# The gates' rank chain of a top-2 mixture of experts: comparisons, maximum and subtraction on VectorE, counts, clipping and sum on GpSimd, the sum folded into the softmax's norm

## The chip, the cores and the metric

One core of a Trainium2 chip. The metric is the device time of one execution in microseconds; 617.84 us is the median of three runs of the kernel before.

## The reference

Inputs r, k, v, w, a, b are float32 [4, 8, 768, 40]. A recurrence over 768 steps gives y, which is laid out as x [4, 768, 320] and goes through a mixture of four attention experts of width 64. Per token the two experts with the largest gate logits count, weighted by a softmax over the two:

```python
def _moe_ref(x, w_gate, wq, wk, wv, wo):
    logits = x @ w_gate                                     # [B, S, 4]
    topk = np.argpartition(-logits, K, axis=-1)[..., :K]    # K = 2
    sel = np.take_along_axis(logits, topk, axis=-1)
    w = np.exp(sel - sel.max(-1, keepdims=True))
    w /= w.sum(-1, keepdims=True) + 1e-09
    for e in range(E):
        # q, k, v = x @ wq[e], x @ wk[e], x @ wv[e]; causal scores; softmax a
        ye = a @ v @ wo[e]
        # out += w of e, where e is one of the two, times ye
```

## The kernel before

The first part (up to about 375 us) computes the recurrence in chunks. The change does not touch it. The second part is the function moe. It works on 4 batches of 768 tokens; a batch has 6 tiles of 128 tokens, and its x comes in two halves of 384 tokens.

**What proj(b) gives per batch.** load (l, L708 to L710) fetches half of x from memory, in three transfers by SyncE's queue. split (s) makes a high and a low part of it: VectorE casts (L716), GpSimd subtracts twice (L717, L718). qk (k) makes the queries or keys of two experts for a half of the tokens: 8 matmuls (L739), a copy by ScalarE (L747), the rest by VectorE (L748), and for keys a transfer (L750). vg (v) makes the values and the gate logits of one tile (L758), which ScalarE copies out of PSUM (L761, and L762 into G[b], the tile "gg").

**The gates before.** rank (r; R for one half of the tiles) compares logit a with those after it on VectorE (L776, into "gc"); one slot later GpSimd adds each comparison to the later experts' counters and subtracts it from the earlier one's (L778, L780, the tile "gr"; set by four memsets, L773). Over a = 0, 1, 2 that makes nine GpSimd instructions. shift (h, H) takes the maximum on VectorE (L784), subtracts it on GpSimd (L785) and turns the counters into zeros and ones on VectorE (L786). gate (g, G) takes the exponential on ScalarE (L789), multiplies by the zeros and ones on GpSimd (L790), sums, adds 1e-9 and inverts on VectorE (L791 to L793) and multiplies on GpSimd (L794). Batch 0 does this by halves of three tiles, the other batches for all six at once, so there are five such chains.

**What a unit does.** A unit is one batch, one pair j of query tiles and one expert e; there are 48. scores: matmuls into PSUM (L816), mask addition and row minimum by VectorE (L823), exponential with its sum by ScalarE (L825). norm: VectorE adds 1e-9 to the sum (L830) and inverts it (L831), GpSimd multiplies by the gate (L832) and multiplies the two tiles of probabilities by that (L836). transp: TensorE transposes the probabilities (L844), ScalarE or VectorE copies them out of PSUM (L850, L848). mix: the product with the values (L862), copied by ScalarE and VectorE (L866, L867). fin: the output projection (L873), its copy (L876) and the store.

**What sets the order.** The program writes slots: the loop over units takes turns between scores, transposes, mixes and the pieces of the next batch's projection, which the strings FIRST, FILL0, FILL1 and FILL list; later(d, f) puts f d slots on (DL, DE, DN, DR). This part is not in manual order: the layer below places each engine's instructions, taking the program's order as the priority and its own idea of when inputs are ready, so that an engine's order in the trace can differ from the program's. Each engine executes its queue in order. Matmul outputs of "pt" share three PSUM buffers.

Of the kernel before, what the change touches and what calls it, by code (L numbers as in the profile page):

```python
# [14 lines left out]
AX = mybir.AxisListType  # L15
# [576 lines left out]

LAG = (3, 4, 6)

DL, DE, DN, DR = 1, 3, 4, 1

FIRST = "l1 k1 v0 k0 s1 v2 v1 R0 R1 R2 k2 H0 k3 G0"
FILL0 = "k4 k7", "k6 v4 k5", "v3", "v5 R3 R4 R5 H1", "G1", "", "", "", "", "", "", ""
FILL1 = "", "l0 s0", "", "", "l1", "k1 k0 s1", "v0 k2 v1 k3", "v3 v4", "v5 v2 k4", "", "r0 r1 k5", "r2 h g k6 k7"
FILL = "l0 s0 l1", "k3", "k0", "v0", "k1 k2", "s1", "v2 v1", "v5 v3 v4 r0", "k4", "r1 r2 k5", "k7 h g k6", ""  # L600
# [67 lines left out]
def moe(tc, ctx, I, xT, out, ident, pre, FL=None, FI=None):  # L668
    nc = tc.nc
    sp = ctx.enter_context(tc.tile_pool(name="moe", bufs=1, reuse_waits="tile"))  # L670
    pp = ctx.enter_context(tc.tile_pool(name="mps", bufs=1, space=PSUM, reuse_waits="tile"))
    V, A, T, PL = nc.vector, nc.scalar, nc.tensor, nc.gpsimd

    def f32(x):
        return x.bitcast(F32)
# [3 lines left out]
    def later(d, f):  # L679
        due.setdefault(now[0] + d, []).append(f)  # L680

    def slot(f):

        now[0] += 1
        for g in due.pop(now[0], []):
            g()
        f()

    def pj():
        return pp.tile([128, 512], F32, name="pt", tag="pt", bufs=3)  # L690
# [7 lines left out]
        A.activation(WS[0].rearrange("p k n -> p (k n)"), x, AF.Copy)  # L698
        V.tensor_tensor(WS[1].rearrange("p k n -> p (k n)"), x, h, op=OP.subtract)

    XH, XL, QS, KS, VV, G = {}, {}, {}, {}, {}, {}

    def load(b, n):

        t = slice(384 * n, 384 * n + 384)
        x = XL[b, n] = sp.tile([128, 3, 384], FR, name="x", bufs=2)
        x = f32(x)
        nc.sync.dma_start(x[:, 0:2], xT[b, 0:256, t].rearrange("(k p) t -> p k t", p=128))  # L708
        nc.sync.dma_start(x[0:64, 2], xT[b, 256:320, t])
        nc.sync.dma_start(x[64:128, 2], xT[b, 256:320, t])  # L710

    def split(b, n):
        l = XL[b, n]
        x = f32(l)
        h = XH[b, n] = sp.tile([128, 3, 384], FR, name="xh", bufs=2)
        V.tensor_copy(h, x)  # L716
        PL.tensor_tensor(h[64:128, 2], x[64:128, 2], f32(h[64:128, 2]), op=OP.subtract)  # L717
        PL.tensor_tensor(l[:, 0:2], x[:, 0:2], f32(h[:, 0:2]), op=OP.subtract)  # L718

    def products(w, x, b, n):  # L720

        h, l = XH[b, n], XL[b, n]
        return [(w[y][:, k], h[:, k]) for y in range(2) for k in range(2)] + [(w[y][:, 2], h[:, 2]) for y in range(2)] + \
               [(w[0][:, k], l[:, k]) for k in range(2)]

    def proj(b):
        wqk = [w.rearrange("p (k m n) -> p k m n", k=3, m=4) for w in WQ]
        wvg = [w.rearrange("p (k n) -> p k n", k=3) for w in WV]

        QS[b] = sp.tile([128, 4, 768], FR, name="qs", bufs=2)  # L730
        KS[b] = sp.tile([128, 4, 2, 768], FR, name="ks", bufs=2)
        VV[b] = sp.tile([128, 6, 4, 64], F32, name="vv", bufs=2)
        G[b] = sp.tile([128, 6, 4], F32, name="gg", bufs=2)
        def qk(m, n):
            def f():
                p = pj()[:, 0:384]
                prs = products([w[:, :, m] for w in wqk], None, b, n)
                for j, (w, x) in enumerate(prs):
                    T.matmul(p, w, x, start=(j == 0), stop=(j == len(prs) - 1))  # L739
                t = slice(384 * n, 384 * n + 384)  # L740
                for s in range(2):
                    e, o, x = 2 * (m % 2) + s, slice(64 * s, 64 * s + 64), slice(64 - 64 * s, 128 - 64 * s)
                    if m < 2:
                        h, l, c = QS[b][o, e, t], QS[b][x, e, t], -0.125
                    else:
                        h, l, c = KS[b][o, e, 0, t], KS[b][o, e, 1, t], 1.0
                    A.activation(h, p[o], AF.Copy, scale=c)  # L747
                    later(DL, lambda h=h, l=l, c=c, o=o: V.scalar_tensor_tensor(l, p[o], c, f32(h), op0=OP.mult, op1=OP.subtract))  # L748
                    if m >= 2:
                        later(DL, lambda e=e, o=o, x=x: nc.sync.dma_start(f32(KS[b][x, e, :, t]), f32(KS[b][o, e, :, t])))  # L750
            return f
        def vg(i):
            def f():
                n, c = divmod(i, 3)
                p = pj()[:, 0:260]
                prs = products(wvg, None, b, n)
                for j, (w, x) in enumerate(prs):
                    T.matmul(p, x[:, 128 * c:128 * c + 128], w, start=(j == 0), stop=(j == len(prs) - 1))  # L758
                v = VV[b][:, i]
                pv = p[:, 0:256].rearrange("p (e d) -> p e d", e=4)  # L760
                A.activation(v, pv, AF.Copy)  # L761
                A.activation(G[b][:, i], p[:, 256:260], AF.Copy)  # L762
            return f
        gs = {}
        def rank(a, i=slice(0, 6)):

            L = G[b][:, i]
            if a == 0:
                gs["R"] = sp.tile([128, 6, 4], F32, name="gr", bufs=2)
                gs["c"] = sp.tile([128, 3, 6, 3], F32, name="gc", bufs=1)  # L770
                gs["m"] = sp.tile([128, 2, 6], F32, name="gm", bufs=2)
                for d in range(4):
                    PL.memset(gs["R"][:, i, d], 3.0 - d)  # L773
            R, c = gs["R"][:, i], gs["c"][:, a, i]
            n = c.shape[1]
            V.tensor_tensor(c[:, :, 0:3 - a], L[:, :, a:a + 1].to_broadcast([128, n, 3 - a]), L[:, :, a + 1:4], op=OP.is_ge)  # L776
            def count():
                PL.tensor_tensor(R[:, :, a + 1:4], R[:, :, a + 1:4], c[:, :, 0:3 - a], op=OP.add)  # L778
                for d in range(3 - a):
                    PL.tensor_tensor(R[:, :, a], R[:, :, a], c[:, :, d], op=OP.subtract)  # L780
            later(DR, count)
        def shift(i=slice(0, 6)):
            L, R, mx = G[b][:, i], gs["R"][:, i], gs["m"][:, 0, i]
            V.tensor_reduce(mx, L, axis=AX.X, op=OP.max)  # L784
            PL.tensor_tensor(L, L, mx[:, :, None].to_broadcast(L.shape), op=OP.subtract)  # L785
            V.tensor_scalar(R, R, 1.5, None, op0=OP.is_lt)  # L786
        def gate(i=slice(0, 6)):
            L, R, mx, c = G[b][:, i], gs["R"][:, i], gs["m"][:, 0, i], gs["m"][:, 1, i]
            A.activation(L, L, AF.Exp)  # L789
            PL.tensor_tensor(L, L, R, op=OP.mult)  # L790
            V.tensor_reduce(mx, L, axis=AX.X, op=OP.add)  # L791
            V.tensor_scalar(mx, mx, 1e-9, None, op0=OP.add)
            V.reciprocal(c, mx)  # L793
            PL.tensor_tensor(L, L, c[:, :, None].to_broadcast(L.shape), op=OP.mult)  # L794
        half = lambda x: slice(3 * x, 3 * x + 3)
        return dict(l=lambda n: load(b, n), s=lambda n: split(b, n), k=lambda i: qk((0, 2, 1, 3)[i % 4], i // 4)(), v=lambda i: vg(i)(),
                    r=rank, h=lambda i: shift(), g=lambda i: gate(), R=lambda x: rank(x % 3, half(x // 3)),
                    H=lambda x: shift(half(x)), G=lambda x: gate(half(x)))

    OT, PT = {}, {}  # L800

    def unit(b, j, e, last):
# [24 lines left out]
                later(DN, norm)  # L827
        def norm():
            m = st["m"]
            V.tensor_scalar(m[:, 2], m[:, 1], 1e-9, None, op0=OP.add)  # L830
            V.reciprocal(m[:, 2], m[:, 2])  # L831
            PL.tensor_tensor(m[:, 3], m[:, 2], G[b][:, 2 * j:2 * j + 2, e], op=OP.mult)  # L832
            for t in range(2):
                n = 128 * (2 * j + t + 1)
                P = st["P"][t]
                PL.tensor_tensor(P[:, 0:n], P[:, 0:n], m[:, 3, t:t + 1].to_broadcast([128, n]), op=OP.mult)  # L836
# [149 lines left out]
```

## Time and profile before

| | |
|---|---|
| median of 3 runs | 617.84 us (616.05 to 618.46) |
| profiled execution, its own time | 615.63 us |
| its span, first to last instruction | 613.4 us |
| TensorE matmul busy | 537.8 us (88%), 8753 instructions |
| VectorE, ScalarE busy | 465.0 us, 469.8 us (76%, 77%) |
| GpSimd busy | 383.5 us (63%), 618 instructions |

The engines are PE (TensorE; PEld its weight loads), DVE (VectorE), ACT (ScalarE), POOL (GpSimd) and SP (SyncE). A row of the order of instructions gives the start in us, the time in us of the group, engine, line, operation, output<-input tiles, shape and count, and in brackets the idle time of the engine before it and who ended it. What matters below is where TensorE is idle, and which engine's wait ends last there.

### The profile page before, as it was taken

How to read it: one execution, taken by the hardware profiler on the slowest of the kernel's cores; microseconds unless marked ns; L12 is line 12 of the kernel's file. 1: busy time of each engine (PE TensorE's matmuls, PEld its weight loads, DVE VectorE, ACT ScalarE, POOL GpSimd, SP SyncE). 2: the span in 40 equal slices, each digit the busy share in tenths (PEclk: the TensorE clock that was granted, in tenths of full speed). 3: DMA queues.
4: the chain of work that ended last, by engine and by line, in shares of the span. 5: the costliest groups of instructions: out<-in, count | busy, mean ns of one | idle time of the engine just before them, and what ended most of it. 6: DMA issues, size and time to landing. Idle time of an engine off the chain costs nothing.

```text
span 613.4 us, 22296 instructions
## 1 busy us (share of the span) xinstructions
PE 537.8 (88%) x8753; PEld 473.7 (77%) x8753; DVE 465.0 (76%) x1142; ACT 469.8 (77%) x1272; POOL 383.5 (63%) x618
## 2 busy tenths in 40 slices
PE   5554589998898899889899999889999889999996
PEld 5554588887777788778788888778988778887884
DVE  7978868899989999997676584777885477567752
ACT  7992479899878988987889985667775567677773
POOL 2421089859988988998984630685763746363851
PEclk9555589999999999999999999999999989999998
DMA  7885244576477557746925845222221131102101
GB/s 189 214 192 135 95 112 123 134 196 161 117 181 196 154 129 206 166 101 173 229 85 157 216 119 162 76 79 66 83 77 48 40 91 59 59 2 57 45 36 52
DMA packets 63690, 73.77 MB, mean 120 GB/s; under 512 B 30168, under 2 KB 48344, under 8 KB 63576
## 3 DMA queue, kind: packets, MB, share of 16 engines
q1 hardware_dynamic: 63432, 72.15, 45.4%
q8 instruction: 72, 1.18, 0.8%
q14 instruction: 42, 0.34, 0.2%
q10 hardware_dynamic: 144, 0.10, 0.1%
HBM read 54.92 MB, written 11.01 MB: 107 GB/s over the span
## 4 chain that ended last, share of the span: by engine, by line
PE 53%; ACT 16%; POOL 11%; DVE 10%; issue 7%; DMA 2%; SPq 1%; POOLq 0%; DVEq 0%; ACTq 0%
PE py L415 6%; PE ot L862 6%; PE pt L739 5%; PE sc L816 4%; PE pt L844 4%; PE pt L873 4%; POOL MT L319 4%; PE pt L441 3%; PE ps L392 3%; POOL TP L319 3%; PE ps L405 3%; PE ps L383 3%; PE pt L758 3%; PE pt L372 2%; ACT GT L386 2%
## 5 line engine op out<-in xcount | busy, mean ns | idle before, releaser
L319 POOL TENSOR_TENSOR MT<-MT,TP 128x30 f32<-128x30 f32 (+9 forms) x150 | 98.2, 654 | 11.6
L319 POOL TENSOR_TENSOR TP<-MT 128x30 f32<-128x30 f32 (+9 forms) x150 | 93.6, 624 | 11.4
L836 POOL TENSOR_TENSOR P<-P,m 128x128 f32<-128x128 f32 (+2 forms) x96 | 89.0, 948 | 3.5
L415 PE MATMUL py<-R,LS 128*40 128x80 f32 x1536 | 83.5, 236 | 1.9 <-DVE R L408 0.4
L823 DVE CUSTOM_DVE_ANT_0 P<-sc,MK 128x128 f32<-128x128 f32 (+2 forms) x96 | 59.5, 622 | 23.6 <-PE sc L816 13.9
L825 ACT ACTIVATE P<-P,m 128x128 f32<-128x128 f32 (+2 forms) x96 | 63.8, 665 | 11.5 <-DVE m L823 10.7
L415 PEld LDWEIGHTS py<-R,LS 128*40 128x40 f32 x1536 | 63.0, 118 | 8.6 <-ACT LS L445 3.6
L408 DVE TENSOR_TENSOR R<-ps,CM 64x128 f32<-64x128 f32 x192 | 55.0, 286 | 16.3 <-PE ps L405 12.3
L816 PE MATMUL sc<-ks,qs 128*128 128x384 f32 (+4 forms) x256 | 61.5, 345 | 2.0 <-DVE m L823 1.9
L394 ACT ACTIVATE R<-ps 32x160 f32<-32x160 f32 x192 | 56.6, 295 | 5.3 <-PE ps L392 1.2
L386 ACT ACTIVATE GT<-ps 32x160 f32<-32x160 f32 x192 | 56.4, 294 | 3.7 <-PE ps L383 0.3
L832 POOL TENSOR_TENSOR m<-m,gg 128x2 f32<-128x2 f32 x48 | 10.3, 214 | 78.0 <-DVE m L831 54.7
L844 PE MATMUL pt<-CM,P 128*128 128x128 f32 x336 | 52.5, 277 | 6.2 <-ACT pt L850 5.1
L445 ACT ACTIVATE LS<-pt 40x320 f32<-40x320 f32 x92 | 39.6, 430 | 12.6 <-PE pt L441 9.3
L392 PE MATMUL ps<-GT,TT 128*33 128x80 f32 x768 | 46.7, 242 | 2.7 <-issue 1.0
L376 ACT ACTIVATE LS<-pt 64x320 f32<-64x320 f32 x96 | 41.4, 432 | 9.7 <-PE pt L372 8.2
L844 PEld LDWEIGHTS pt<-CM,P 128*128 128x128 f32 x336 | 40.1, 141 | 11.2 <-ACT pt L850 6.2
L405 PE MATMUL ps<-RB,VU 128*64 128x64 f32 x768 | 46.0, 228 | 2.0 <-ACT VU L400 1.5
L816 PEld LDWEIGHTS sc<-ks,qs 128*128 128x128 f32 x256 | 40.8, 191 | 4.2 <-DVE m L823 3.4
L739 PE MATMUL pt<-xh,wq 128*128 128x384 f32 x192 | 41.6, 349 | 2.1 <-DVE xh L716 1.2
L283 PE MATMUL ps<-AB,KB 40*64 40x32 f32 x512 | 26.1, 273 | 19.0 <-DVE AB L258 12.8
L441 PE MATMUL pt<-CM,R 104*104 104x104 f32 x368 | 42.4, 258 | 0.0
(160 smaller groups left out, 1337.6 us busy)
## 6 DMA issues: line engine op xcount, KB each, us to landing
RB<-in_RB SPq DMA_DIRECT2D x24, 320.0 KB
EK<-in_EK SPq DMA_DIRECT2D x18, 416.0 KB
ks<-ks SPq DMA_DIRECT2D x32, 192.0 KB
R<-in_VG SPq DMA_DIRECT2D x24, 208.0 KB
EW<-in_EA SPq DMA_DIRECT2D x18, 214.5 KB
R<-in_VT SPq DMA_DIRECT2D x48, 80.0 KB
R<-in_RT SPq DMA_DIRECT2D x24, 160.0 KB
xT<-XT SPq DMA_DIRECT2D x48, 80.0 KB
```

The lines of the kernel that those rows point to most:

```text
L319: return [lambda: e.tensor_tensor(tmp, row, col, op=OP.mult), lambda: e.tensor_tensor(o, o, tmp, op=OP.add)]
L386: A.activation(gt[b:b + 32, s::2], p_g[64 * s:64 * s + 32], AF.Copy)
L392: T.matmul(p_u[64 * x:64 * x + 33, y], tt[:, o:o + 33], gt[:, 2 * p:2 * p + 2], start=True, stop=True, tile_position=(0, 64 * x))
L405: T.matmul(p_f[64 * x:64 * x + 64, y], vu[:, p, :], rb[:, 4 * g + p, :], start=True, stop=True, tile_position=(0, 64 * x))
L415: T.matmul(py[64 * s:64 * s + 40, p], ls[:, h, :], m, start=True, stop=True, tile_position=(0, 64 * s))
L441: T.transpose(PT[0:104, P // 4, 104 * (P % 4):104 * (P % 4) + 104], rn[0:104, o:o + 104], ident[0:104, 0:104])
L739: T.matmul(p, w, x, start=(j == 0), stop=(j == len(prs) - 1))
L816: T.matmul(ps[:, c, 0:cw], QS[b][:, e, o], KS[b][:, e, z, k], start=(z == 0), stop=(z == 1))
L823: V.tensor_tensor_reduce(pv, ps[:, 0:ch, 0:cw], MK[:, 768 - n:768].rearrange("p (c k) -> p c k", c=ch), 1.0, 3e38, OP.add, OP.min, m[:, 0, ...
L825: later(DE, lambda: A.activation(P[:, 0:n], P[:, 0:n], AF.Exp, bias=m[:, 0, t:t + 1], scale=-1.0, accum_out=m[:, 1, t:t + 1]))
L836: PL.tensor_tensor(P[:, 0:n], P[:, 0:n], m[:, 3, t:t + 1].to_broadcast([128, n]), op=OP.mult)
L844: T.transpose(p[:, 128 * y:128 * y + 128], st["P"][t][:, 128 * c:128 * c + 128], ident)
```

## The change

- rank keeps only the comparison; the counters start at d - 1 and not at 3 - d, and the delay DR is gone.
- shift takes the maximum and subtracts it on VectorE, takes the exponential on ScalarE at once, and then does all nine counts on GpSimd, with the signs turned round, and clips the counters to 0 and 1 there (max(min(R, 1), 0)).
- gate is GpSimd's alone: product, two additions for the sum over four experts, and an instruction that adds 1e-9 and writes the sum to a new tile "gt" (GS[b], two buffers). The gates are no longer divided by their sum.
- norm multiplies the softmax's sum (plus 1e-9) by that sum of the gates before it inverts, in place of adding 1e-9 alone.
- The tiles "gr" and "gm" have one buffer and not two.
- FIRST, the order of batch 0's first pieces, has v1 k2 k3 v2 and then the ranks, where it had v2 v1, the ranks, and k2 and k3 among the rest.

```diff
-DL, DE, DN, DR = 1, 3, 4, 1
-FIRST = "l1 k1 v0 k0 s1 v2 v1 R0 R1 R2 k2 H0 k3 G0"
+DL, DE, DN = 1, 3, 4
+FIRST = "l1 k1 v0 k0 s1 v1 k2 k3 v2 R0 R1 R2 H0 G0"
...
+        GS[b] = sp.tile([128, 6], F32, name="gt", bufs=2)
         def rank(a, i=slice(0, 6)):
...
-                gs["R"] = sp.tile([128, 6, 4], F32, name="gr", bufs=2)
+                gs["R"] = sp.tile([128, 6, 4], F32, name="gr", bufs=1)
                 gs["c"] = sp.tile([128, 3, 6, 3], F32, name="gc", bufs=1)
-                gs["m"] = sp.tile([128, 2, 6], F32, name="gm", bufs=2)
+                gs["m"] = sp.tile([128, 2, 6], F32, name="gm", bufs=1)
                 for d in range(4):
-                    PL.memset(gs["R"][:, i, d], 3.0 - d)
...
+                    PL.memset(gs["R"][:, i, d], d - 1.0)
+            c = gs["c"][:, a, i]
+            V.tensor_tensor(c[:, :, 0:3 - a], L[:, :, a:a + 1].to_broadcast([128, c.shape[1], 3 - a]), L[:, :, a + 1:4], op=OP.is_ge)
         def shift(i=slice(0, 6)):
             L, R, mx = G[b][:, i], gs["R"][:, i], gs["m"][:, 0, i]
             V.tensor_reduce(mx, L, axis=AX.X, op=OP.max)
-            PL.tensor_tensor(L, L, mx[:, :, None].to_broadcast(L.shape), op=OP.subtract)
-            V.tensor_scalar(R, R, 1.5, None, op0=OP.is_lt)
+            V.tensor_tensor(L, L, mx[:, :, None].to_broadcast(L.shape), op=OP.subtract)
+            A.activation(L, L, AF.Exp)
+            for a in range(3):
+                c = gs["c"][:, a, i]
+                PL.tensor_tensor(R[:, :, a + 1:4], R[:, :, a + 1:4], c[:, :, 0:3 - a], op=OP.subtract)
+                for d in range(3 - a):
+                    PL.tensor_tensor(R[:, :, a], R[:, :, a], c[:, :, d], op=OP.add)
+            PL.tensor_scalar(R, R, 1.0, 0.0, op0=OP.min, op1=OP.max)
         def gate(i=slice(0, 6)):
-            A.activation(L, L, AF.Exp)
+            L, R, t, g = G[b][:, i], gs["R"][:, i], gs["m"][:, :, i], GS[b][:, i]
             PL.tensor_tensor(L, L, R, op=OP.mult)
-            V.tensor_reduce(mx, L, axis=AX.X, op=OP.add)
-            V.tensor_scalar(mx, mx, 1e-9, None, op0=OP.add)
-            V.reciprocal(c, mx)
-            PL.tensor_tensor(L, L, c[:, :, None].to_broadcast(L.shape), op=OP.mult)
+            PL.tensor_tensor(t.rearrange("p k i -> p i k"), L[:, :, 0:2], L[:, :, 2:4], op=OP.add)
+            PL.tensor_tensor(g, t[:, 0], t[:, 1], op=OP.add)
+            PL.tensor_scalar(g, g, 1e-9, 1.0, op0=OP.add, op1=OP.mult)
...
         def norm():
             m = st["m"]
-            V.tensor_scalar(m[:, 2], m[:, 1], 1e-9, None, op0=OP.add)
+            V.scalar_tensor_tensor(m[:, 2], m[:, 1], 1e-9, GS[b][:, 2 * j:2 * j + 2], op0=OP.add, op1=OP.mult)
             V.reciprocal(m[:, 2], m[:, 2])
```

## Rows read from the trace of the kernel before

**Rows 1.** Stretches: length, busy PE PEld DVE ACT POOL, PEclk, DMA share, GB/s.
```profile
396.00:404.00 8.00, 5.21 (x34) 4.13 (x32) 4.62 (x22) 4.92 (x18) 7.28 (x24) 1.00 0.44 125
432.00:480.00 48.00, 47.24 (x347) 41.42 (x347) 34.75 (x86) 33.38 (x83) 26.81 (x33) 1.00 0.25 72
493.80:497.30 3.50, 3.50 (x16) 3.50 (x15) 2.42 (x9) 3.05 (x8) 2.03 (x4) 0.51 0.02 5
```

**Rows 2.** Order of instructions: the memsets of the counters of batch 0.
```profile
370.09 0.32 POOL L773 MEMSET gr<- 128x3 f32 x8 [3.44 <-PE ps L392]
```

**Rows 3.** Waits from 376 us on: who for whom; us, times, longest.
```profile
ACT gg L789 <- POOL gg L785: 9.2, 4, 4.4
DVE gr L786 <- POOL gr L780: 8.6, 4, 3.6
```

**Rows 4.** Order of instructions, TensorE: idle times near the five gate chains.
```profile
384.99 0.77 PE L739 MATMUL pt<-xh,wq 128*128 128x384 f32 x3 [1.21 <-DVE xh L716]
...
388.21 0.62 PE L739 MATMUL pt<-x,wq 128*128 128x384 f32 x2 [1.27 <-DVE gm L792]
...
404.09 0.73 PE L816 MATMUL sc<-ks,qs 128*128 128x512 f32 x2 [1.65 <-DVE m L823]
...
427.34 0.55 PE L844 MATMUL pt<-CM,P 128*128 128x128 f32 x3 [1.04 <-ACT pt L850]
...
492.35 0.55 PE L844 MATMUL pt<-CM,P 128*128 128x128 f32 x3 [3.67 <-ACT pt L850]
...
549.18 0.55 PE L844 MATMUL pt<-CM,P 128*128 128x128 f32 x3 [0.38 <-ACT pt L850]
```

**Rows 5.** Order of instructions, VectorE and GpSimd: batch 0's first half.
```profile
383.97 0.17 DVE L786 TENSOR_SCALAR gr<-gr 128x12 f32<-128x12 f32 x1 [1.60 <-POOL gr L780]
384.08 0.76 DVE L716 CAST xh<-x 128x1152 fp32r<-128x1152 f32 x1
...
385.26 1.01 POOL L717 TENSOR_TENSOR xh<-x,xh 64x384 fp32r<-64x384 f32 x1
386.34 1.81 POOL L718 TENSOR_TENSOR x<-x,xh 128x768 fp32r<-128x768 f32 x1
```

**Rows 6.** The same: batch 0's second half.
```profile
400.67 0.97 POOL L836 TENSOR_TENSOR P<-P,m 128x128 f32<-128x128 f32 x2
...
403.26 0.17 DVE L786 TENSOR_SCALAR gr<-gr 128x12 f32<-128x12 f32 x1 [2.58 <-POOL gr L780]
...
405.56 0.14 DVE L830 TENSOR_SCALAR m<-m 128x2 f32<-128x2 f32 x1
```

**Rows 7.** The same, GpSimd and ScalarE: batch 1.
```profile
423.20 2.68 POOL L836 TENSOR_TENSOR P<-P,m 128x640 f32<-128x640 f32 x2
...
426.44 0.22 ACT L789 ACTIVATE gg<-gg 128x24 f32<-128x24 f32 x1 [1.73 <-POOL gg L785]
```

**Rows 8.** The same: batch 2, with TensorE's instructions that come next.
```profile
489.13 0.53 POOL L780 TENSOR_TENSOR gr<-gr,gc 128x6 f32<-128x6 f32 x3
...
489.87 0.22 ACT L789 ACTIVATE gg<-gg 128x24 f32<-128x24 f32 x1 [4.41 <-POOL gg L785]
...
491.99 1.82 POOL L836 TENSOR_TENSOR P<-P,m 128x384 f32<-128x384 f32 x2
...
495.17 1.08 PE L844 MATMUL pt<-CM,P 128*128 128x128 f32 x4
...
504.64 0.86 PE L816 MATMUL sc<-ks,qs 128*128 128x320 f32 x4
```

**Rows 9.** Lines L830, L776 (ns min/median/max); VectorE beside GpSimd, batch 1.
```profile
L830 DVE TENSOR_SCALAR m<-m x48: 126/169/1426, 391.2 to 599.7; 128x2 f32<-128x2 f32 x48
L776 DVE TENSOR_TENSOR gc<-gg x15: 151/164/626, 382.0 to 544.9; 128x6 f32<-128x6 f32 x5, 128x18 f32<-128x18 f32 x3, 128x12 f32<-128x12 f32 x3, 128x9 f32<-128x9 f32 x2
...
429.67 1.01 POOL L717 TENSOR_TENSOR xh<-x,xh 64x384 fp32r<-64x384 f32 x1
...
429.73 0.98 DVE L792 TENSOR_SCALAR gm<-gm 128x6 f32<-128x6 f32 x1
```

More of the change, by code (lines that the diff above doesn't have):

```diff
@@ L699, in split_wo @@
         V.tensor_tensor(WS[1].rearrange("p k n -> p (k n)"), x, h, op=OP.subtract)
-    XH, XL, QS, KS, VV, G = {}, {}, {}, {}, {}, {}
+    XH, XL, QS, KS, VV, G, GS = {}, {}, {}, {}, {}, {}, {}
     def load(b, n):
@@ L768, in rank @@
             if a == 0:
-                gs["R"] = sp.tile([128, 6, 4], F32, name="gr", bufs=2)
+                gs["R"] = sp.tile([128, 6, 4], F32, name="gr", bufs=1)
                 gs["c"] = sp.tile([128, 3, 6, 3], F32, name="gc", bufs=1)
-                gs["m"] = sp.tile([128, 2, 6], F32, name="gm", bufs=2)
+                gs["m"] = sp.tile([128, 2, 6], F32, name="gm", bufs=1)
                 for d in range(4):
-                    PL.memset(gs["R"][:, i, d], 3.0 - d)
[L774 to L781, printed above, removed]
+                    PL.memset(gs["R"][:, i, d], d - 1.0)
+            c = gs["c"][:, a, i]
+            V.tensor_tensor(c[:, :, 0:3 - a], L[:, :, a:a + 1].to_broadcast([128, c.shape[1], 3 - a]), L[:, :, a + 1:4], op=OP.is_ge)
         def shift(i=slice(0, 6)):
@@ L784, in shift @@
             V.tensor_reduce(mx, L, axis=AX.X, op=OP.max)
-            PL.tensor_tensor(L, L, mx[:, :, None].to_broadcast(L.shape), op=OP.subtract)
-            V.tensor_scalar(R, R, 1.5, None, op0=OP.is_lt)
+            V.tensor_tensor(L, L, mx[:, :, None].to_broadcast(L.shape), op=OP.subtract)
[6 more added lines that the diff above has]
+            PL.tensor_scalar(R, R, 1.0, 0.0, op0=OP.min, op1=OP.max)
         def gate(i=slice(0, 6)):
-            L, R, mx, c = G[b][:, i], gs["R"][:, i], gs["m"][:, 0, i], gs["m"][:, 1, i]
-            A.activation(L, L, AF.Exp)
+            L, R, t, g = G[b][:, i], gs["R"][:, i], gs["m"][:, :, i], GS[b][:, i]
             PL.tensor_tensor(L, L, R, op=OP.mult)
-            V.tensor_reduce(mx, L, axis=AX.X, op=OP.add)
-            V.tensor_scalar(mx, mx, 1e-9, None, op0=OP.add)
-            V.reciprocal(c, mx)
-            PL.tensor_tensor(L, L, c[:, :, None].to_broadcast(L.shape), op=OP.mult)
+            PL.tensor_tensor(t.rearrange("p k i -> p i k"), L[:, :, 0:2], L[:, :, 2:4], op=OP.add)
+            PL.tensor_tensor(g, t[:, 0], t[:, 1], op=OP.add)
+            PL.tensor_scalar(g, g, 1e-9, 1.0, op0=OP.add, op1=OP.mult)
         half = lambda x: slice(3 * x, 3 * x + 3)
```

## The prediction

> **What bounds the kernel now.** I read the stretches of the attention part first, then the trace's order of instructions, then the waits, then TensorE's idle times, and last the instructions around each of the five places where gates are computed. In the stretches [rows 1] the reader should see that TensorE is the bound wherever no gate is computed: 47.24 us busy of 48.00 from 432 to 480. Where gates are computed it is not: 5.21 of 8.00 from 396 to 404. So a microsecond of idle TensorE removed there is a microsecond off the end, as long as nothing else is late at the same place.
>
> [Rows 2] show that the trace's order is not the program's: the memsets of both halves' counters run at 370.09, though the second half's stand several units further down in the program. The layer that builds this part places an instruction where it thinks its inputs are ready, earlier program lines first. The order after the change can therefore only be argued, not read off the diff.
>
> The waits [rows 3] name the price of the gates today. ScalarE waits 9.2 us, four times, with its exponential of the gates for GpSimd's subtraction of the maximum. VectorE waits 8.6 us, four times, with the comparison on L786 for GpSimd's counts. Everything behind these two in the queues waits too: copies of transposes out of PSUM (L850), mask additions of scores (L823), the cast of the next x (L716). TensorE's idle times [rows 4] lie just there: 1.21 + 1.27 in the start, 1.65 for the second half of batch 0, 1.04, 3.67 and 0.38 for batches 1, 2 and 3; 9.22 together. After the 3.67 the granted clock is 0.51 over 493.8 to 497.3 [rows 1], that is nearly all at the lower level, 1.2 GHz; over 396 to 404, and so up to the idle time of 1.65, it was 1.00, 2.4 GHz.
>
> **The change part by part.** *Start of batch 0* [rows 5]. The cast of the second half of x ran at 384.08, right behind L786, which had waited 1.60 for GpSimd. L786 is gone, and the ranks move behind v2 in the program, so the cast can start when VectorE is free, at 383.97 - 1.60 = 382.37, 1.7 earlier, and some 0.4 more since the three comparisons and the maximum no longer stand ahead of it. I take 2.0. GpSimd's two splits of x (1.01 and 1.81) follow the cast, and TensorE's wait at 388.21 ends with the second, at 388.15; both come 2.0 earlier. The bounds are 0 (x's load may land as late as the cast; no row shows its landing) and 2.48, the two idle times themselves. I take 2.0 since L786's wait ended within 0.11 us of the cast. The order v1, k2, k3, v2 is the same TensorE work: 0.
>
> *Second half of batch 0* [rows 6]. VectorE stood from 400.68 to 403.26 before L786, while the mask addition that TensorE waits for stood behind it. Without L786 it starts some 2 us earlier, TensorE had nothing else from 402.44: 1.65 gained, bounds 0 and 1.65. *Batch 1* [rows 7]. The exponential stood 1.73 before 426.44, until GpSimd had done a pair of probabilities of 2.68; it now waits for VectorE's own subtraction, so the copy behind it, and TensorE's 1.04, are free. Bounds 0 and 1.04; I take 1.04, since TensorE's next input, that pair, was ready at 425.88.
>
> *Batch 2* [rows 8]. The exponential waited from 485.46 to 489.87. From its start to TensorE's next transposes, which want the copy behind it, is 492.35 - 489.87 = 2.48 [rows 4, 8]. If it starts at 486.3 they can run at 488.8; TensorE left off at 492.35 - 3.67 = 488.68, so almost all of the 3.67 goes. Next late is GpSimd: its counts end at 489.13 + 0.53 = 489.66; clip, product, two sums and the final scaling take five more at about 0.2 (three counts take 0.53), to 490.7, where today it passes through the subtraction, two waits on other engines and L794, and starts the next pair at 491.99. That pair can start at 490.9 and end at 492.7 instead of 493.81. TensorE's transposes that want it, at 495.17 today, would be reached near 491 and wait to 492.7: 2.5 gained. A wait of 1 to 2 us is nearer to the 1.65 that left the clock at 1.00 than to the 3.67, so I count the clock as kept: from 495.17 to 497.3 some 2.1 us of work at half rate give back 1.0. Together 3.5; bounds 1.1 (GpSimd's own gain) and 5.4 (3.67, and half of 3.5 at the lower clock). *Batch 3*: 0.38, bounds 0 and 0.38 [rows 4].
>
> *What is added.* GpSimd has two instructions more for each of five gates (clip, two sums, final scaling; less the subtraction and one product): 5 x 2 x 0.2 = 2.0 us, beside TensorE's work except in batch 2, where it is in the sum; bounds 0 and 2.0. The counters' single buffer keeps the next memset behind the product that frees it; both are GpSimd's, so no engine waits. VectorE loses five instructions per gate and gains one subtraction. The norm's L830 becomes an instruction with two tensors: its median is 169 ns and that of L776, also two tensors on few columns, 164 [rows 9]: 0. It adds one wait: every norm now needs the gates' sum from GpSimd, and behind it in VectorE's queue stand mask additions and copies. For batch 2 the first norm that reads its sum comes after its first scores, at 504.64 [rows 8], over 10 us after the sum. For the second half of batch 0 it is close: GpSimd is through with a pair at 400.67 + 0.97, counts (1.5) and five more (1.0) make 404.2, and the norm of the first unit that needs it ran at 405.56 [rows 6]. Both move up, the norm by 1.65 more, which makes a wait of 0.3 at most: 0, bound 0.3.
>
> [Rows 9] also show VectorE's two-input and plain instructions stretched while GpSimd works: L792 took 0.98 inside GpSimd's 1.01. By that, VectorE's new subtraction can be stretched by as much as one GpSimd instruction, which is why I let batch 2's exponential start at 486.3 and not at 485.46 and the 0.2 of a subtraction: half a split like that of 1.81 [rows 5] may lie before it. The Trainium skill, page "SBUF — State Buffer", section "Who interferes with whom", says that a VectorE instruction with two SBUF inputs and a GpSimd instruction that reads SBUF exclude each other; by that rule the stretch is a full block, in all five places. The trace agrees: L776, with two such inputs, takes up to 0.626 where its median is 0.164; what it would cost here is a rival below.
>
> **The sum**: 2.0 + 1.65 + 1.04 + 3.5 + 0.38 = 8.6 us. The profiled execution took 615.63 (span 613.4), so its successor would take 607.0, span about 604.8. The median of the three runs, 617.84, is 2.2 above it; off the median the forecast is 609.2.
>
> **Rivals.** *GpSimd counts first.* The layer puts the start's counts ahead of the x split, so the reordering does not do what it says. The ranks stand behind v2, whose matmuls end where TensorE left off today, 383.78; counts from about 384.9, 1.5 + 0.2, then 1.01 + 1.81: TensorE's wait ends near 389.5, 1.3 later than now and not 2.0 earlier. Gain 8.6 - 3.3 = 5.3: 612.5. For it: today's order has the counts ahead of the split; against it: the split is now much earlier in the program than the counts.
>
> *The block.* VectorE's subtraction waits out a GpSimd instruction in all five places, near 0.9 each (half of a split, 1.81 [rows 5]): gain 8.6 - 4.5 = 4.1: 613.7. Against it: batch 2's delay is in the sum already. The rule that speaks for it is that of the Trainium skill, page "SBUF — State Buffer", named above.
>
> *Nothing to be had.* Where the stall goes, the next input is just as late: GpSimd's pairs of probabilities, or the placing differs and puts a like idle elsewhere. What stays is GpSimd's 1.1 in batch 2 and about 0.9 in batch 1: 615.8. For it: GpSimd is busy 7.28 of 8.00 around 400 [rows 1].
>
> *The wait is only renamed (slower).* VectorE now stands at the norm for GpSimd's sum as long as it stood at L786. This decides if GpSimd takes the gates' block behind the next pair of probabilities (2.68 [rows 7]) so that the sum comes after VectorE has reached a norm that reads it, the second half of batch 0 above all. Then nothing is gained, two more GpSimd instructions in five places cost 2.0, and one pair 2.7: 622.5. Against it: batches 1 to 3 have their sums long before.
>
> **How the numbers follow.** Forecast 0.58; counts first 0.11; the block 0.08; nothing 0.14; renamed 0.09. The likeliest gives 609.2. Its own range is 606 (nearly all upper bounds: 2.48 + 1.65 + 1.04 + 5.4 + 0.38 = 10.95, and 1 for a better order) to 613. The whole range reaches up to 616.5, which takes in 612.5, 613.7 and 615.8, and leaves out 622.5; down to 605.5. A measurement here can tell about 0.5%, 3.1 us: under 614.8 is faster, 0.58 + 0.11 + 0.08 = 0.77; same 0.14; slower 0.09.
>
> **What would show it.** Right: no wait of ScalarE's exponential or VectorE on GpSimd's gates; TensorE's idle before 388 and near 402 and 426 gone; near 490 at most 2 us, with the clock at 1.00. Wrong in the start: the cast still follows the comparisons, or GpSimd's split follows counts. Wrong in batch 2: TensorE still idle 3 us or more. Wrong in sign: VectorE's norm waits for a tile of gates' sums, several us in all.

## The result, and the profile after

The changed kernel is faster by 1.0%: 610.99 us, the median of 20 runs, against 617.0 for the kernel before on the same chips (20 runs); the ratio is 0.9901, with a 95% interval of 0.9879 to 0.9923. That is 6.0 us by the medians, where the forecast was 8.6. The single executions lie between 606.12 and 616.06. The ratios, here and in the table of the experiments, leave out executions over 1.5% above the fastest of the same kernel (one of the 20 of after, five of the 12 of "clip only", one each of "old order" and of "the same, subtraction apart"), while the medians hold all.

| | before | after |
|---|---|---|
| median of 20 runs, us | 617.0 | 610.99 |
| span of the profiled execution, us | 613.4 | 610.7 |
| start of the last matmul of the recurrence (L415) in it | 374.8 | 376.4 |
| from there to the end of the span | 238.6 | 234.3 |

The profiled pair shows less than the medians, and the last two rows say in part why. The recurrence, which the change does not touch, took 1.6 us more in the execution shown of after: behind the stretch from 15 to 81 us, nearly all of it at 0.5 in both, TensorE's granted clock fell to 0.5 there twice, for 3.4 us at 264.1 and at 308.5, and never in the one shown of before. So I compare the part behind the recurrence, which I call *the tail* (the expectations below call it the part after the attention): 238.6 and 234.3 us, 4.3 us less. Where the rest of the 6.0 lies no trace shows. Where in the tail the time went is seen from when a given matmul of the mix (L861, L862 before) starts, counted from the last one of the recurrence:

| start of the mix matmul number | 1 | 121 | 145 | 345 | end of the span |
|---|---|---|---|---|---|
| before | 30.62 | 104.94 | 127.29 | 219.57 | 238.57 |
| after | 28.91 | 102.78 | 124.00 | 215.48 | 234.32 |
| gained so far | 1.7 | 2.2 | 3.3 | 4.1 | 4.3 |

Number 1 lies behind TensorE's idle times at both halves of batch 0's gates, number 121 behind batch 1's, number 145 behind batch 2's and number 345 behind batch 3's. From 121 to 145, over the gates of batch 2, which were to bring 3.5, the gain is 1.1.

The page of the kernel after; the first row is busy time, share of the span and instructions of each engine, the second the granted clock in 40 slices:

```profile
PE 540.2 (88%) x8753; PEld 475.8 (78%) x8753; DVE 467.3 (77%) x1127; ACT 469.5 (77%) x1272; POOL 384.7 (63%) x628
...
PEclk9555589999999999989989999999999989999999
```

Stretches of the kernel after: length, busy PE PEld DVE ACT POOL, PEclk, DMA share, GB/s:

```profile
396.00:404.00 8.00, 6.82 (x47) 5.74 (x45) 7.05 (x28) 6.33 (x23) 7.30 (x18) 1.00 0.54 145
432.00:480.00 48.00, 47.28 (x350) 41.44 (x350) 33.88 (x84) 33.67 (x84) 27.54 (x32) 1.00 0.25 72
489.40:492.80 3.40, 3.40 (x17) 2.52 (x16) 3.25 (x10) 3.04 (x10) 2.57 (x11) 0.50 0.01 2
```

They answer to [rows 1]. Around batch 0's second half TensorE is now busy for 6.82 of 8.00 us, where it was 5.21. From 432 to 480 nothing changed, as nothing should. Behind batch 2's gates the clock is still at its lower level, 1.2 GHz: 0.50 for 3.4 us.

Waits of the kernel after from 376 us on: who for whom, line that wrote it; us, times, longest:

```profile
DVE m L829 <- POOL gt L793: 2.3, 2, 2.0
ACT gg L781 <- DVE gg L780: 2.3, 2, 1.8
```

These are what is left of [rows 3]. ScalarE's 9.2 us for GpSimd's subtraction and VectorE's 8.6 us for GpSimd's counts have no successors among the waits for gates; instead VectorE's norm waits twice for the gates' sum, and ScalarE twice for VectorE's subtraction.

TensorE in the kernel after, its idle times of over 0.4 us in the tail (start, busy time, engine, line, instruction, idle time before it and what ended it):

```profile
386.12 0.41 PE L739 MATMUL pt<-xh,wq 128*128 128x384 f32 x1 [0.74 <-DVE xh L716]
...
389.08 0.61 PE L739 MATMUL pt<-x,wq 128*128 128x384 f32 x2 [1.20 <-POOL x L718]
...
393.59 0.96 PE L758 MATMUL pt<-wv,xh 128*128 128x260 f32 x6 [0.66 <-DVE qs L748]
...
399.39 0.99 PE L758 MATMUL pt<-wv,xh 128*128 128x260 f32 x6 [0.47 <-ACT gg L762]
...
403.98 0.73 PE L815 MATMUL sc<-ks,qs 128*128 128x512 f32 x2 [0.55 <-DVE m L822]
...
414.44 0.63 PE L843 MATMUL pt<-CM,P 128*128 128x128 f32 x4 [0.41 <-POOL P L835]
...
488.44 0.73 PE L815 MATMUL sc<-ks,qs 128*128 128x512 f32 x2 [2.04 <-DVE m L822]
...
497.96 0.79 PE L739 MATMUL pt<-xh,wq 128*128 128x384 f32 x3 [0.60 <-DVE pt L847]
...
553.17 1.31 PE L739 MATMUL pt<-xh,wq 128*128 128x384 f32 x6 [0.60 <-DVE pt L847]
```

Beside [rows 4]: 1.21 and 1.27 became 0.74 and 1.20, with 0.66 new behind them; 1.65 became 0.55; 1.04 and 0.38 are gone; 3.67 became 2.04, and what it waits for is new: not ScalarE's copy but VectorE's mask addition (L822). The 0.60 at 497.96 is new too. An idle time of before that [rows 4] do not show, ahead of the 1.65, is gone as well:

```profile
399.92 0.33 PE L844 MATMUL pt<-CM,P 128*128 128x128 f32 x1 [0.61 <-POOL P L836]
```

VectorE of the kernel after in the start:

```profile
384.06 1.12 DVE L748 SCALAR_TENSOR_TENSOR qs<-pt,qs 64x384 fp32r<-64x384 f32 x2 [0.39 <-ACT qs L747]
385.22 0.76 DVE L716 CAST xh<-x 128x1152 fp32r<-128x1152 f32 x1
...
391.92 0.16 DVE L829 SCALAR_TENSOR_TENSOR m<-m,gt 128x2 f32<-128x2 f32 x1 [1.97 <-POOL gt L793]
```

Against [rows 5] the cast no longer follows a wait for GpSimd, but it follows a split of qs; and the first norm stands 1.97 us for the gates' sum. The cast did not stand for x's load: in the trace each transfer raises a semaphore 16 times as it lands, and by these counts the last of the load's three had landed at 383.95, 1.27 us ahead of the cast (before: 381.54, cast at 384.08).

VectorE and GpSimd at the 2.04, batch 2 of the kernel after (its three comparisons are one row), and TensorE's scores that the mask addition of 512 columns takes up:

```profile
480.71 0.16 DVE L829 SCALAR_TENSOR_TENSOR m<-m,gt 128x2 f32<-128x2 f32 x1 [1.28 <-ACT P L824]
480.95 0.76 DVE L716 CAST xh<-x 128x1152 fp32r<-128x1152 f32 x1
481.63 0.16 DVE L830 RECIPROCAL m<-m 128x2 f32<-128x2 f32 x1
...
484.05 3.65 DVE L776 TENSOR_TENSOR gc<-gg 128x18 f32<-128x18 f32 x3
487.62 0.17 DVE L779 TENSOR_REDUCE gm<-gg 128x6 f32<-128x24 f32 x1
487.70 0.67 DVE L822 CUSTOM_DVE_ANT_0 P<-sc,MK 128x512 f32<-128x512 f32 x1
488.31 0.08 DVE L822 DVE_READ_ACCUMULATOR2_ANT m<- 128x1 f32 x1
488.31 0.23 DVE L780 TENSOR_TENSOR gg<-gg,gm 128x24 f32<-128x24 f32 x1
...
481.95 1.01 POOL L717 TENSOR_TENSOR xh<-x,xh 64x384 fp32r<-64x384 f32 x1 [1.72 <-DVE m L830]
483.04 0.20 POOL L831 TENSOR_TENSOR m<-m,gg 128x2 f32<-128x2 f32 x1
483.19 1.85 POOL L718 TENSOR_TENSOR x<-x,xh 128x768 fp32r<-128x768 f32 x1
484.99 2.68 POOL L835 TENSOR_TENSOR P<-P,m 128x640 f32<-128x640 f32 x2
487.63 0.22 POOL L784 TENSOR_TENSOR gr<-gr,gc 128x18 f32<-128x18 f32 x1
...
483.50 0.71 PE L815 MATMUL sc<-ks,qs 128*128 128x512 f32 x2
```

The same comparisons in the kernel before, with GpSimd's order there, and in batch 3 of the kernel after:

```profile
484.59 0.79 DVE L776 TENSOR_TENSOR gc<-gg 128x18 f32<-128x18 f32 x3
...
481.98 3.20 POOL L836 TENSOR_TENSOR P<-P,m 128x640 f32<-128x640 f32 x2
485.26 1.02 POOL L717 TENSOR_TENSOR xh<-x,xh 64x384 fp32r<-64x384 f32 x1
...
543.10 0.34 DVE L776 TENSOR_TENSOR gc<-gg 128x18 f32<-128x18 f32 x3
```

The three comparisons are the same instructions as before, and took 3.65 us where they had taken 0.79. Taken one by one they run 484.05 to 485.07, 484.99 to 486.27 and 486.19 to 487.69. GpSimd's x split ends at 485.04, and its pair of probabilities is two instructions that end at 486.24 and 487.67: each comparison ends with one GpSimd instruction. Behind them stand the mask addition, whose scores had been done since 484.21, and, behind that, TensorE.

### The profile page after: what moved, and what is told of

Its sections match the earlier page's. It is cut to its first block, busy times and chain, and to the rows that moved or that the text cites. A ratio compares the mean times of both kernels' runs of the same rounds, so it can differ in the third digit from the quotient of the medians.

```text
span 610.7 us, 22319 instructions
## 1 busy us (share of the span) xinstructions
PE 540.2 (88%) x8753; PEld 475.8 (78%) x8753; DVE 467.3 (77%) x1127; ACT 469.5 (77%) x1272; POOL 384.7 (63%) x628
## 4 chain that ended last, share of the span: by engine, by line
PE 53%; POOL 16%; DVE 13%; ACT 9%; issue 6%; DMA 2%; SPq 1%; DVEq 0%; POOLq 0%; ACTq 0%
POOL MT L319 7%; POOL TP L319 7%; PE ot L861 6%; PE py L415 6%; PE pt L739 5%; PE sc L815 5%; PE pt L843 4%; PE pt L872 4%; PE pt L441 4%; PE pt L758 3%; PE ps L392 3%; PE ps L405 3%; PE ps L383 3%; PE pt L372 2%; PE ps L399 2%
## 5 line engine op out<-in xcount | busy, mean ns | idle before, releaser
L415 PE MATMUL py<-R,LS 128*40 128x80 f32 x1536 | 84.0, 238 | 2.2 <-DVE R L408 0.4
L822 DVE CUSTOM_DVE_ANT_0 P<-sc,MK 128x128 f32<-128x128 f32 (+2 forms) x96 | 59.3, 623 | 24.1 <-PE sc L815 12.4
L415 PEld LDWEIGHTS py<-R,LS 128*40 128x40 f32 x1536 | 63.6, 119 | 8.7 <-ACT LS L445 3.6
```

The lines of the kernel that those rows point to most:

```text
L415: T.matmul(py[64 * s:64 * s + 40, p], ls[:, h, :], m, start=True, stop=True, tile_position=(0, 64 * s))
L822: V.tensor_tensor_reduce(pv, ps[:, 0:ch, 0:cw], MK[:, 768 - n:768].rearrange("p (c k) -> p c k", c=ch), 1.0, 3e38, OP.add, OP.min, m[:, 0, ...
```

## The experiments

The theory that I took into the runs: the waits went as foretold, and batch 2 lost its gain since VectorE's comparisons are held by GpSimd's instructions. Its rivals: the new order of the start does the work; the fold (norm times the gates' sum) costs what the rest gains; what is left is set by x's load. The table holds all runs. Ratios are against runs of the kernel before on the same chip, whose medians were 617.99 to 619.18 beside the other kernels, and are not the quotients of two medians; "idle" is TensorE's first idle time over 0.5 us around batch 2's gates, "clock" whether the granted clock fell to 0.5 there.

| kernel | median | ratio (95%) | tail | idle | clock | three comparisons |
|---|---|---|---|---|---|---|
| before | 617.0 | | 238.6 | 3.67 | fell | 0.79 |
| after | 610.99 | 0.9901 (0.9879 to 0.9923) | 234.3 | 2.04 | fell | 3.65 |
| order only | 618.98 | 1.0002 (0.9969 to 1.0035) | 240.6 | 3.67 | fell | 0.77 |
| old order | 612.94 | 0.9868 (0.9818 to 0.9919) | 237.2 | 2.23 | fell | 3.83 |
| comparisons on GpSimd | 616.98 | 0.996 (0.9929 to 0.9991) | 237.8 | 2.80 | fell | on GpSimd |
| the same, subtraction apart | 611.36 | 0.9899 (0.9869 to 0.9929) | 234.5 | 0.83 | kept | on GpSimd |
| not folded | 611.2 | 0.9872 (0.9821 to 0.9924) | 233.3 | 0.93 | kept | 0.88 |
| inverted by GpSimd | 610.32 | 0.9897 (0.9855 to 0.9938) | 231.1 | 0.80 | kept | 0.74 |
| subtraction only | 616.2 | 0.9974 (0.9939 to 1.0009) | 235.9 | 2.56 | fell | 0.76 |
| clip only | 617.81 | 0.9961 (0.9921 to 1.0001) | 237.8 | 3.54 | fell | 0.66 |
| wo later | 613.48 | 0.9921 (0.9887 to 0.9955) | 233.9 | 0.75 | kept | 2.35 |
| inverted, wo later | 610.0 | 0.9851 (0.9801 to 0.9901) | 232.8 | 0.72 | kept | 0.65 |
| inverted, compared on GpSimd, apart | 611.66 | 0.9893 (0.9854 to 0.9932) | 230.9 | 0.93 | kept | on GpSimd |

The tail is one execution's, and a fall of the clock in the start alone moves it: "order only" has one at 406.7, "old order" one of 6.8 us at 387.9.

**Comparisons on GpSimd.** After, with this edit:

```
-            V.tensor_tensor(c[:, :, 0:3 - a], ..., L[:, :, a + 1:4], op=OP.is_ge)
+            PL.tensor_tensor(c[:, :, 0:3 - a], ..., L[:, :, a + 1:4], op=OP.subtract)
+            PL.tensor_scalar(c[:, :, 0:3 - a], c[:, :, 0:3 - a], 0.0, None, op0=OP.is_ge)
```

> The changed kernel with its three comparisons per gate chain taken off VectorE: GpSimd subtracts and compares with 0, so two GpSimd instructions stand for one of VectorE's (six for three). Theory (the block): VectorE's comparisons, with two inputs in SBUF, stood behind GpSimd's instructions for 3.65 us in batch 2 and 1.94 us in the start, and TensorE's idle 2.04 us near 488 with the low clock behind it comes from that. Then the mask addition of 512 columns follows its predecessor in batch 2 at once, the 2.04 is gone or under 0.7, the clock stays at 1.00 there, and the time is 2 to 4 us under the changed kernel's 611. Rival (GpSimd is late anyway): the idle time only moves to GpSimd's later counts and pairs, TensorE still idles 2 us near there, and the time is that of the changed kernel or up to 2 us more, for six more GpSimd instructions of 0.2 in each of five places.

It lost most of the gain, which neither the theory nor the rival had in its range. VectorE of this kernel, batch 2:

```profile
487.23 0.17 DVE L780 TENSOR_REDUCE gm<-gg 128x6 f32<-128x24 f32 x1
491.54 0.18 DVE L781 TENSOR_TENSOR gg<-gg,gm 128x24 f32<-128x24 f32 x1 [4.13 <-POOL gc L776]
491.64 0.68 DVE L823 CUSTOM_DVE_ANT_0 P<-sc,MK 128x512 f32<-128x512 f32 x1
```

VectorE's subtraction writes over the logits, so it now has to wait until GpSimd's comparisons have read them: 4.13 us, and the mask addition waits behind it. The run took one hold away and put another in its place, so it tells nothing of the first; the next run mends that.

**The same, with the subtraction into a tile of its own.**

```
+        GE[b] = sp.tile([128, 6, 4], F32, name="ge", bufs=2)
...
-            V.tensor_tensor(L, L, mx[:, :, None].to_broadcast(L.shape), op=OP.subtract)
-            A.activation(L, L, AF.Exp)
+            X = GE[b][:, i]
+            V.tensor_tensor(X, L, mx[:, :, None].to_broadcast(L.shape), op=OP.subtract)
+            A.activation(X, X, AF.Exp)
```

> The run before this with comparisons on GpSimd, but the maximum's subtraction writes a tile of its own, in which the exponential and the gates then live, so that VectorE's subtraction no longer has to wait until GpSimd has read the logits (4.13 us in batch 2, 1.86 us in the start). Theory (the block, by comparisons): with neither comparisons nor that wait on VectorE, the idle time of TensorE in batch 2, 2.04 us with the changed kernel and 2.80 with comparisons on GpSimd, falls under 0.7, and the part after the attention takes 2 to 3 us less than the changed kernel's 235. Rival (GpSimd is late anyway): 2 us of idle time stay in batch 2, now for GpSimd's pairs. In the start the first norm's wait for the gates' sum stays at about 3 us, which takes back up to 1.5 us either way.

With no comparison on VectorE, batch 2's idle time is 0.83 (0.96 a little later), not under 0.7, and the clock stays at 1.00. From mix matmul 121 to 145 it takes 19.29 us, after 21.22, before 22.35: 3.1 less than before, near the 3.5 foretold for batch 2. Here VectorE's subtraction itself is held, by one split that ends at 486.19:

```profile
485.12 1.11 DVE L783 TENSOR_TENSOR ge<-gg,gm 128x24 f32<-128x24 f32 x1
```

The start pays: its GpSimd chain is longer by the comparisons, the first norm waits for it, and TensorE stands 1.74 us at 393.54 (0.66 in after), with the clock down from 394.7. Tail and median come out as in after; the 2 to 3 us expected of the tail are not there.

**Not folded.** After, with the gates divided by their sum again, the reciprocal on VectorE, and the norm of before:

```
+            V.reciprocal(g, g)
+            PL.tensor_tensor(L, L, g[:, :, None].to_broadcast(L.shape), op=OP.mult)
...
-            V.scalar_tensor_tensor(m[:, 2], m[:, 1], 1e-9, GS[b][:, 2 * j:2 * j + 2], op0=OP.add, op1=OP.mult)
+            V.tensor_scalar(m[:, 2], m[:, 1], 1e-9, None, op0=OP.add)
```

> The changed kernel with the fold undone: VectorE inverts the gates' sum, GpSimd multiplies the gates by it, and the norm adds 1e-9 alone as before. Theory (the fold only moves a wait): the wait of 1.97 us of the first norm for the gates' sum leaves VectorE's queue, five inversions and five products come back; the time is within 1.5 us of the changed kernel. Rival (the fold brings the gain): 3 us or more slower than the changed kernel. Second rival (the fold's new wait costs): 1 to 2 us faster, TensorE's idle near 389 to 394 smaller by 1 us.

The comparisons stay on VectorE, yet take 0.88. What differs is GpSimd's order: here the pair of probabilities (485.34, 2.68 us) stands ahead of the split (488.10). The wait for the sum is only moved to the reciprocal: 5.9 us in five places, the longest 2.0.

**The old order.** After, with the order string of before:

```
-FIRST = "l1 k1 v0 k0 s1 v1 k2 k3 v2 R0 R1 R2 H0 G0"
+FIRST = "l1 k1 v0 k0 s1 v2 v1 R0 R1 R2 k2 H0 k3 G0"
```

> The changed kernel with the old order of batch 0's first pieces (v2 v1, ranks, k2, H0, k3). Theory (the order brings little, since the cast still comes behind the split of k2's queries): TensorE's idle in the start within 1 us of the changed kernel's 0.74 + 1.20 + 0.66, the time within 1 us of it. Rival (the order is what frees the start): 2 us more idle, 2 us slower than the changed kernel.

**The order only.** The kernel before with the new order string (the same edit, the other way round).

> The kernel before with only the new order of batch 0's first pieces; its gates are as before, the long waits of VectorE and ScalarE for GpSimd too. Theory (little from the order): within 1 us of the kernel before, TensorE's 3.67 in batch 2 still there. Rival (the order frees the start): 2 us faster than before.

The order by itself brings nothing that the runs can tell: 1.0002, and a 2.00 us idle time at 405.66 in place of the 1.65 of [rows 4]. Without it the rest of the change holds its gain in the runs (0.9868), though in the profile its start is worse than after's by 2.6 us, 31.48 against 28.91 to the first mix matmul, with the clock down for 6.8 us. There the cast ran at 383.20, right behind the landing of x (383.05), but GpSimd did its counts and the gate first and split x only at 386.46, and TensorE stood 1.90 us for that: the rival "GpSimd counts first", under the old order. So in the start the order helps only together with the other parts, and the intervals do not tell its worth from nothing.

**The subtraction only**, in the kernel before:

```
-            PL.tensor_tensor(L, L, mx[:, :, None].to_broadcast(L.shape), op=OP.subtract)
+            V.tensor_tensor(L, L, mx[:, :, None].to_broadcast(L.shape), op=OP.subtract)
```

> The kernel before with one edit: the maximum's subtraction on VectorE. ScalarE's exponential no longer waits for GpSimd (9.2 us, four times, before); VectorE's comparison with 1.5 on L786 still waits for the counts (8.6 us). Theory (both waits carry the stalls): TensorE's 1.04 in batch 1 goes (it hung on ScalarE alone), the 3.67 in batch 2 shrinks little, since VectorE's mask addition stands behind L786: 1 to 2 us faster than before. Rival (ScalarE's wait is all of it): 5 to 6 us faster, as fast as the changed kernel.

**The clip only**, in the kernel before (counters start at d - 1, counts with signs turned):

```
-            V.tensor_scalar(R, R, 1.5, None, op0=OP.is_lt)
+            PL.tensor_scalar(R, R, 1.0, 0.0, op0=OP.min, op1=OP.max)
```

> The kernel before with one edit: the counters' comparison with 1.5 on VectorE becomes clipping on GpSimd (counts with the signs turned). VectorE no longer waits for the counts there, but L791, the gates' sum, still waits for GpSimd's product; ScalarE's exponential still waits for GpSimd's subtraction. Theory (both waits carry the stalls): 1.65 in batch 0's second half goes, 1.04 and most of 3.67 stay: 1 to 3 us faster than before. Rival (VectorE's wait is all of it): 5 to 6 us faster.

The two halves of the mechanism part in the traces. With VectorE's subtraction the 1.04 of batch 1 is gone, 3.67 is 2.56, 1.65 is 1.48, and VectorE still waits 7.3 us, four times, for the counts. With the clip on GpSimd the 1.65 is gone, 1.04 stays and 3.67 is 3.54; VectorE's wait for the counts has become one of 7.4 us, three times, for GpSimd's product (L791 for L790). Tails: 2.7 and 0.7 less than before; the ratio of neither excludes 1, and the median of "clip only" is that of the kernel before (617.81 against 618.01 on its chip).

**wo later.** After, with the load of wo issued behind the three loads of x's second half:

```
-    nc.sync.dma_start(WO, I["WO"])
...
+        if k == 0:
+            nc.sync.dma_start(WO, I["WO"])
```

> The changed kernel with one load moved: the output projection's weights (320 KB) are issued behind the load of the second half of x and not ahead of it. Theory (the cast in the start waits for its place behind k2's split, and that place comes from x's expected arrival): x arrives about 1 us earlier, the cast comes ahead of the split of k2's queries, TensorE's 0.74 goes and its 1.20 shrinks; the part after the attention is 0.5 to 1.5 us shorter than the changed kernel's 235. Rival (its place does not depend on the arrival): the same order, the same idle times, the same time.

VectorE of this kernel in the start:

```profile
386.34 0.76 DVE L715 CAST xh<-x 128x1152 fp32r<-128x1152 f32 x1 [2.82 <-DMA x<-xT]
```

Here VectorE was free 2.82 us before the cast and stood for the load, whose three pieces were issued from 378.60 on: 7.7 us from the first issue to the cast. In after they were issued from 378.31 on, and the cast ran at 385.22, 6.9 later. The cast did come ahead of the split of k2's queries, as the theory had it, but x did not come earlier: by the semaphore counts its last transfer landed at 386.21, 9.1 us behind the recurrence, in after 7.5. In that transfer the last of 16 counts came 1.9 us behind the one before it; why is open. At batch 2 this kernel is folded like after, but the cast of the next x itself waited for its load (0.18), and the comparisons hit less of GpSimd's work: 2.35 us for the three, 0.75 idle, clock kept.

**Inverted by GpSimd.** After, not folded, with GpSimd raising the sum to the power of -1 (NEG is a column of -1), so that VectorE waits for no gate at all:

```
+            PL.tensor_tensor(g, g, NEG.to_broadcast(g.shape), op=OP.pow)
+            PL.tensor_tensor(L, L, g[:, :, None].to_broadcast(L.shape), op=OP.mult)
```

and the norm as under "not folded".

> The changed kernel with the fold undone and the inversion on GpSimd too (a power of -1, then the product with the gates), so VectorE waits for GpSimd's gates nowhere. Theory (the fold's wait costs little): the wait of 1.97 us in VectorE's queue near 390 is gone, TensorE's idle 0.66 near 393 too, and the time is within 1 us of the changed kernel. Rival: the start gets 1.5 us shorter and the time 1.5 us less.

VectorE and GpSimd of this kernel, batch 2, and TensorE's idle time there:

```profile
479.44 0.17 DVE L833 TENSOR_SCALAR m<-m 128x2 f32<-128x2 f32 x1 [1.27 <-ACT P L828]
479.65 0.17 DVE L834 RECIPROCAL m<-m 128x2 f32<-128x2 f32 x1
479.75 0.76 DVE L718 CAST xh<-x 128x1152 fp32r<-128x1152 f32 x1
...
482.78 0.74 DVE L778 TENSOR_TENSOR gc<-gg 128x18 f32<-128x18 f32 x3
...
480.65 2.68 POOL L839 TENSOR_TENSOR P<-P,m 128x640 f32<-128x640 f32 x2
483.41 1.01 POOL L719 TENSOR_TENSOR xh<-x,xh 64x384 fp32r<-64x384 f32 x1
...
488.10 1.31 PE L741 MATMUL pt<-xh,wq 128*128 128x384 f32 x6 [0.80 <-DVE qs L750]
```

The reciprocal stands right behind the norm here, and the cast behind both; in after the cast stands between them, and GpSimd, which needs the reciprocal for the pair, takes the split first. Now the first comparison is held for 0.58 us, to the end of the pair (483.33), and the other two follow in 0.16 us more, about where the split starts (483.41). From mix matmul 121 to 145 it takes 18.57 us (after 21.22), and the first mix matmul comes at 28.16 (after 28.91), since the first norm does not wait for the sum. The tail, 231.1, is 3.2 shorter than after's; the ratios, 0.9897 and 0.9901, do not tell the two apart.

**Inverted, wo later** and **inverted, compared on GpSimd, apart** put the edits above together.

> The kernel with the inversion on GpSimd and no fold, with that load moved too. If both gains add, it is 0.5 to 1.5 us under the one with the inversion alone, whose part after the attention took 231: 229.5 to 230.5, a time near 609. If the load's place does not matter, the same as that one.

> Comparisons on GpSimd with a tile of their own for the gates, and the inversion on GpSimd, no fold: VectorE is left with the maximum and the subtraction. Theory (the block no longer costs once the x split stands behind the pair of probabilities): no better than the kernel with the inversion alone, and 0.5 to 1.5 us worse in the start, where GpSimd's chain is 1.2 us longer. Rival (VectorE's stretched comparisons still cost in the start, 1.94 us there): 1 us better.

Neither adds anything that the runs can tell: the first keeps a 2.25 us idle time in the start (tail 232.8, where 229.5 to 230.5 was expected), the second brings 1.27 back at 551.51. The three versions that invert on GpSimd lie with after at 610 to 612.

## Why the prediction was right, and where it was not

Sign and range held, and the mechanism in part: the waits it named are gone, and 610.99 lies between 605.5 and 616.5, near its 609.2. The sum was too large, 8.6 against 6.0 by the medians and 4.3 in the profiled pair; that the time came so near owes something to luck, since two of the terms, with 5.5 of the 8.6, brought about 1. Two of its own signs failed too: idle times before 388 stayed (0.74, 1.20), and near 490 the clock fell behind 2.04 us. By its terms:

- **Start, 2.0, and second half of batch 0, 1.65.** Together 1.7 instead of 3.65, by the table of mix matmuls. By TensorE's idle times the start brought nothing: 2.48 before, 2.60 after with the new 0.66. Its term failed at "the cast can start when VectorE is free": it came 8.8 us behind the recurrence (385.22 less 376.43), before 9.3 (384.08 less 374.82), so 0.5 earlier and not 2.0. The load, which the prediction had as its lower bound, was not the reason: it had landed 7.5 us behind the recurrence, early enough for 1.6 of the 2.0 or so. A split of qs (384.06, 1.12 us) had been placed ahead of the cast, and the sum has no term for what the layer places there. The second half brought what was foretold, though not only where: 1.10 of the 1.65, and the 0.61 at 399.92, less 0.1 at 399.39 (0.38 there before). VectorE's comparisons took 0.92 there beside GpSimd, 0.71 before.
- **Batch 1, 1.04.** The idle time is gone, and "subtraction only" shows which edit does it. But the net between mix matmuls 1 and 121 is 0.5: a new idle time of 0.41 came up at 414.44, where transposes wait for GpSimd's probabilities.
- **Batch 2, 3.5.** It brought 1.1, and here 2.4 of the shortfall lie. That 1.1 is also the lower bound is chance: the bound was GpSimd's earlier pair, the measured value is, to 0.1, the 3.67 that became 2.04, less the new 0.60 at 497.96. The step that failed is "if it starts at 486.3". The prediction let VectorE's new subtraction be held by half a split. The subtraction took 0.23, but it began at 488.31 only, and the exponential, by then behind other work of ScalarE, at 491.22; held were the three comparisons ahead of it, unchanged instructions that had taken 0.79, by a split and both halves of a pair. Its second step failed with it: 2.04 us idle brought the clock down, though the prediction had put 1 to 2 us nearer to the 1.65 that left it up. With the comparisons' hold cut short by GpSimd's other order, or gone since they were moved, the stretch from 121 to 145 is 18.57 ("inverted") or 19.29 ("apart") instead of 22.35: 3.8 or 3.1 us, about the 3.5 foretold.
- **Batch 3, 0.38.** It brought 0.8 between 145 and 345. TensorE's idle time there fell by the 0.4 foretold; the other 0.4 is not idle time, and no run shows its cause.
- **Added work, 0 to 2.0 on GpSimd; the norm, 0.** The pages bear out GpSimd's ten instructions more (628 for 618), not VectorE's count: it loses four per gate and gains one (1127 for 1142), not five. The two-tensor norm costs what the old one did: median 161 ns, 169 before [rows 9]. Its wait at the second half of batch 0 is 0.31, the bound named (0.3). Not foreseen is the first norm of all, which stood 1.97 us for the sum at 391.92 and cost TensorE the 0.66 at 393.59; that is the rival "only renamed", in one place. "Inverted" takes this wait away, and the 0.66 with it.

The block stood among the rivals as one on VectorE's subtraction, in all five places, 0.9 each. It came on the comparisons, above all in one place: in the start they took 1.94, but there the first norm waits for GpSimd's counts and sum, which stood behind the same split. At batch 2 three comparisons ended with three GpSimd instructions, 3.65 us for what takes 0.34 in batch 3 (543.10), where GpSimd had just ended a pair and had nothing next. The Trainium skill, page "SBUF — State Buffer", section "Who interferes with whom", says that a VectorE instruction with two SBUF inputs and a GpSimd instruction that reads SBUF exclude each other; these rows agree with it.

How long the hold is depends on GpSimd's order, and that went with the norm. At batch 2, in all five kernels with the folded norm, the cast stands between norm and reciprocal and GpSimd takes the split first; in all eight with the norm of before the reciprocal comes first, then the pair, and comparisons on VectorE take 0.65 to 0.88 there. "Not folded" differs from after in the fold alone, so here the fold, which saves a reciprocal and a product per gate, sets up the hold. It is not the hold alone that costs: "wo later" has comparisons of 2.35 us and 0.75 idle. Why the layer that places instructions answers to the norm in this way was not tried and stays open.

## What to carry to other kernels

Moving an operation off the engine that waits for it pays at most up to the next late input, so look that one up first: here it was an instruction placed ahead of the one that was to come earlier, and at batch 2 unchanged instructions that had become slow. Where an instruction with two SBUF inputs runs on VectorE beside a busy GpSimd, count the whole GpSimd instructions that can hold it, for the unchanged instructions too, since an edit elsewhere can change GpSimd's order under them. An update in place makes the writer wait for readers on another engine (4.13 us in "comparisons on GpSimd"); a tile of its own for the result took that wait away.

## What the runs showed of the hardware beyond that

An instruction of 0.16 us can take ten times as long by where it falls: VectorE's comparisons in after took from 0.15 to 1.78. An instruction with one input can be held too, as the norm of "inverted" was (median 0.17) by a split that ended at 486.32:

```profile
485.10 1.25 DVE L833 TENSOR_SCALAR m<-m 128x2 f32<-128x2 f32 x1 [0.64 <-ACT P L828]
```

Idle times of TensorE of 2.04 to 3.67 around batch 2 were each followed by a granted clock of 0.5 for 3.4 us, those of 0.72 to 0.93 in no kernel; in the start it was less regular: 1.74 at 393.54 was followed by a fall, 2.32 at 388.40 ("wo later") by none. GpSimd's power on 128x6 took 1.33 to 1.36 us, its sums of that size 0.2 (once 0.72 in each of two runs).
